# Weights of a column transform by one radix-two step, and the opening of the kernel in a new order

## The chip, the cores and the metric

The kernel runs on one core of one Trainium2 chip. The metric is device time in microseconds (us) for one execution of the whole program. The engines are named as in the profile: PE is TensorE's matmuls and PEld its weight loads, DVE is VectorE, ACT is ScalarE, POOL is GpSimd, and SP is SyncE, which only issues DMAs. "SPq", "ACTq" and "POOLq" are DMA issues on the queues of those engines.

## The reference

```python
def _attn_ref(x):                                  # x: 8 x 3008 x 256
    X = np.fft.fft(x, axis=1)
    X = np.fft.fft(X, axis=2)
    return X.real.astype(np.float32)

def _moe_ref(x, w_in, w_out):                      # w_in: 256 x 2048, w_out: 2048 x 256
    h = x @ w_in
    g = h * np.cos(h)
    return (g @ w_out).astype(np.float32)

def reference(x, moe_w_in, moe_w_out):
    X = _attn_ref(x)                               # real part of a 2-D transform of each batch
    return _moe_ref(X.reshape(8 * 3008, 256), moe_w_in, moe_w_out)
```

A two-dimensional Fourier transform (along the sequence and along the 256 columns), its real part, and then two matrix products with g = h cos(h) between them. All is float32.

## The kernel before, in words

**The column transform is put into the weights.** The transform along the 256 columns is linear, so the kernel does not apply it to the data: it multiplies w_in by the matrix of cosines and sines once, at the start. The results are WC (cosine part) and WS (sine part), each 128 x 2048. Because of the symmetry of the cosine only 128 of the 256 output columns d are kept, and the data z is folded to the same 128 columns. The remaining column, d = 128, gives one extra row of weights; it is computed in row 0 of WS (the sine of d = 0 is nothing). This row has to become a column: tile `wn` (128 x 16) holds it with the hidden units on the partitions. `send_wn` stores 512 of its elements to DRAM (tile `wd`) and then clears row 0 of WS on POOL; `load_wn` loads them back, element by element, spread over the partitions. Until it is there, `seed` (on ACT) cannot start a step that uses it.

The weights are made in four quarters of 512 hidden units. `load_w(q)` brings a quarter of w_in as two halves of 128 rows each (tile `wr`), `weights(e, q)` multiplies both halves by the table CS and adds them up in one PSUM bank (two matmuls, e = 1 for sine, 0 for cosine), and `keep_weights` copies the bank to WS or WC. The quarter 0 is made before the main loop, quarter 1 partly before it, and quarters 2 and 3 inside its first half-steps.

**The sequence transform** of a batch goes in two stages. In the opening, for batch 0, `fold` adds and subtracts mirrored columns of x (DVE), `first_half` multiplies by small tables into the bank `pz`, ACT copies the bank to `zs`, `store_z` writes it to DRAM (`zd`) and `load_z` reads it back in another order as `z`. `second_half` then makes `pb`, which ACT copies to `pq`, the input of the main loop. For later batches the same is done beside the main loop: `fold_x`, `pair_half`, `keep_z` (an ACT copy from PSUM), `fold_z` (one POOL operation for sums, one for differences), `store_pair`, `load_z`.

**The main loop** runs over 384 steps (8 batches x 6 groups of up to 256 positions x 8 blocks of 256 hidden units); each step has two half-steps of 128 hidden units. A half-step makes h with two matmuls (`mm1` with WC and WS, onto a bank that `seed` has prepared), and then ACT and DVE compute g (`act_e`, `dve_h`, `act_round`, `dve_frac`, `act_sin`, `dve_g`). Per step POOL forms combinations of g (`sums`, tile S), and seven matmuls (`mm2`) multiply g and S by w_out or by combinations of w_out (tile VX, made by `combine_w2` on POOL). The second product of a step follows its first by five half-steps.

**What sets the order.** Everything is in a hand-written order: each engine and each DMA queue runs its instructions in the order in which the program issues them (the program turns the automatic scheduler off), and waits between engines are by semaphore. So an instruction that waits holds up all that stands behind it on its engine or queue. `keep_busy` issues matmuls whose result nobody uses.

In the opening POOL's stream holds, in this order: loads of x and CS, small copies, a load of a piece of BJ, the load of w_in's quarter 1, the loads of the first half of z, the clearing of row 0 of quarter 0, the first two loads of w_out (`load_w2(0, 2)` and `(2, 4)`), the clearing of row 0 of quarter 1, and then `combine_w2`. SP's stream holds the x loads, the stores of z, quarter 0, its share of the z loads, quarter 2, `wn` of quarter 0, quarter 3, and then the rest of z's stores, w_out, BJ and z.

Of the kernel before, what the change touches and what calls it, by code (L numbers as in the profile page):

```python
# [33 lines left out]
def _consts():  # L34
# [57 lines left out]

    c = np.arange(ND)
    d = np.arange(128)
    ang = 2.0 * np.pi * np.outer(c, d) / ND
# [36 lines left out]
def kernel(  # L132
# [88 lines left out]

    CS = cpool.tile([128, 512], FP, tag="CS", name="CS")
    wr = {
# [4 lines left out]
    def raw(q, i):  # L228
        return wr[q][:, 512 * i : 512 * i + 512]
# [6 lines left out]
    def load_cs(eng):  # L236
        eng.dma_start(
            out=CS.rearrange("p (i d) -> p i d", i=2),
            in_=CS_dr.ap().rearrange("(i p) d -> p i d", p=128),
        )  # L240

# [24 lines left out]
    for c in parts[:2]:  # L266
        load_x(c, 1, nc.scalar)
    WC = cpool.tile([128, NDFF], FP, tag="WC", name="WC")
    WS = cpool.tile([128, NDFF], FP, tag="WS", name="WS")
# [43 lines left out]
    def first_half(c):  # L313
# [34 lines left out]
        nc.scalar.copy(out=zps[p][:, 512 * q : 512 * q + 512], in_=pz)  # L348

# [37 lines left out]
    def fold_ends(e):  # L387
        lo, hi = xz[:, 1:128], xz[:, 255:128:-1]
        at = 129 if e else 1
        nc.gpsimd.tensor_tensor(  # L390
            out=xzf[:, at : at + 127], in0=lo, in1=hi, op=ALU.subtract if e else ALU.add
        )
        if e:
            small.append(dict(out=xzf[:, 0:129:128], in_=xz[:, 0:129:128]))
# [12 lines left out]
    def keep_z(b, p, q, pz):  # L407
        if q == 0:
            zrs[b, p] = spool.tile([128, XP * ND], FP, tag="xp", bufs=4, name="zr")
        nc.scalar.copy(out=zrs[b, p][:, 512 * q : 512 * q + 512], in_=pz)  # L410

    def fold_z(b, p, e):
        if e == 0:
            zfs[b, p] = spool.tile([128, 1024], FP, tag="zs", bufs=2, name="zs")
        zr = zrs[b, p][:, 0:1024].rearrange("y (i d) -> y i d", d=ND)
        zv = zfs[b, p].rearrange("y (e i d) -> y e i d", e=2, d=128)
        nc.gpsimd.tensor_tensor(
            out=zv[:, e, :, 1:128],
            in0=zr[:, :, 1:128],
            in1=zr[:, :, 255:128:-1],  # L420
            op=ALU.subtract if e else ALU.add,
        )

# [66 lines left out]
    def load_z(b, half, j0=0, j1=NJ, engs=(nc.sync, nc.sync)):  # L490
        if b not in z2s:
            z2s[b] = spool.tile([128, NJ * 128], FP, tag="z2", bufs=1, name="z2")
        for e in range(2):
            for r in range(2):
                p0 = 64 * e + 32 * half + 16 * r
                f0 = 256 * j0 + r * 128 * (j1 - j0)
# [93 lines left out]

    def weights(e, n, tag="M", pw=None, both=(0, 1)):
        pw = pw or psum("pw", tag)
        for i in both:
            nc.tensor.matmul(  # L594
                pw,
                lhsT=CS[:, 256 * i + 128 * e : 256 * i + 128 * e + 128],
                rhs=raw(n, i),
                start=(i == 0),
                stop=(i == 1),
            )  # L600
        return pw
# [4 lines left out]

    wds = {}

    def send_wn(n):
        row = WS[0:1, 512 * n : 512 * n + 512]  # L610
        wds[n] = dpool.tile([1, 512], FP, tag="wd", bufs=3, name="wd")
        nc.scalar.dma_start(out=wds[n], in_=row)
        nc.gpsimd.memset(row, 0.0)

    def load_wn(n, eng=nc.sync):
        eng.dma_start(
            out=wn[:, 4 * n : 4 * n + 4], in_=wds[n].rearrange("o (k p) -> (o p) k", p=128)
        )

    class Step:  # L620
        pass

    VX = cpool.tile([128, 4 * 1024], FP, tag="VX", name="VX")
    ident = cpool.tile([128, 128], FP, tag="ident", name="ident")
# [296 lines left out]
    copy_v = nc.vector.tensor_copy  # L921
    pds = [psum("pd", tag) for tag in ("H", "H", "M")]
    for pd in pds:
# [44 lines left out]
    for half in range(2):  # L968
        load_z(0, half, 4)
    nc.sync.dma_start(out=L2, in_=L2_dr.ap())  # L970
    opening = {
        0: ((combine_w2, 0, 2), (combine_w2, 2, 4)),
        2: ((load_bj, 512, NJ * 64),),
        3: ((combine_w2, 4, 6, 0, 2),),
        4: ((combine_w2, 4, 6, 2, 4),),
        5: ((combine_w2, 6, 8, 0, 2),),
# [25 lines left out]
    pbs = [psum("pb", "M"), borrow("pb", 1)]  # L1002
# [138 lines left out]
```

## Time and profile before

| | us |
|---|---|
| median of three runs (1918.94 to 1920.99) | 1919.08 |
| the profiled execution, its own time | 1920.06 |
| span of the profiled execution | 1918.3 |
| last matmul starts before / first DMA issue of the last output | 1912.7 / 1913.0 |
| first 26.8 us: TensorE busy | 22.8 |
| 26.8 to 54 us: TensorE busy | 25.7 of 27.2 |
| 54 to 110 us: TensorE busy | 56.0 of 56.0 |

The span is the time from the first to the last instruction that the profiler recorded. "Busy" of an engine is the time in which it has an instruction at work; since matmuls overlap, a busy TensorE is not one at its peak, but idle time of TensorE is time in which nothing was there for it to do. The groups of instructions that cost most of TensorE's time are the second product (L778) and the first (L687):

```profile
L778 PE MATMUL M<-S,VX 128*128 128x256 f32 (+1 forms) x2304 | 626.2, 377 | 0.0
L687 PE MATMUL H<-pq,WC 128*128 128x256 f32 (+1 forms) x1536 | 452.7, 376 | 1.5 <-ACT H L668 1.5
L687 PE MATMUL H<-pq,WS 128*128 128x256 f32 (+1 forms) x1536 | 450.9, 375 | 0.0
```

A row reads: line, engine, operation, output<-inputs, shapes, count, then busy us and mean ns of one, then the idle time of the engine just before them and what ended it. A float32 matmul shows as two records.

### The profile page before, as it was taken

What the parts mean: (1) busy time and instruction counts of PE and PEld (TensorE: products, weight loads), DVE (VectorE), ACT (ScalarE), POOL (GpSimd) and SP (SyncE); (2) the same over time, 40 slices, a digit from 0 to 9 for tenths busy, and PEclk for the clock granted to TensorE, in tenths of its full rate; (3) what the DMA queues carried; (4) which work ended last, traced back from release to release, by engine and by line L of the source; (5) the groups of instructions that cost most, each with busy time, mean ns of one, the idle gap of its engine ahead of it and who ended that gap; (6) DMA issues with size and microseconds to landing.
All of it is one profiled execution on the core that took longest, in us unless ns stands there. A gap on an engine that the chain in (4) does not pass through costs nothing.

```text
span 1918.3 us, 32225 instructions
## 1 busy us (share of the span) xinstructions
PE 1906.3 (99%) x10392; PEld 1660.1 (87%) x10392; DVE 1463.5 (76%) x2538; ACT 1494.6 (78%) x3354; POOL 1431.4 (75%) x1711
## 2 busy tenths in 40 slices
PE   9999999999999999999999999999999999999998
PEld 5888889888888889888898888988889888898887
DVE  5777777777777787777777777777777777788787
ACT  3777778778787787778777787778777887788775
POOL 5778768887688776887668776788867788666775
PEclk9999999999999999999999999999999999999999
DMA  7712225022240223311242212512116121210001
GB/s 214 158 29 37 46 55 127 19 42 39 66 110 19 41 42 95 78 32 33 37 115 61 38 25 42 137 35 42 28 34 151 24 41 26 40 24 15 12 15 30
DMA packets 172811, 108.11 MB, mean 56 GB/s; under 512 B 113506, under 2 KB 152256, under 8 KB 171572
## 3 DMA queue, kind: packets, MB, share of 16 engines
q1 hardware_dynamic: 168612, 101.75, 23.8%
q0 software_dynamic: 1120, 3.01, 0.5%
q10 hardware_dynamic: 2912, 1.29, 0.3%
q8 instruction: 84, 1.38, 0.3%
q14 instruction: 83, 0.68, 0.1%
HBM read 68.72 MB, written 48.40 MB: 61 GB/s over the span
## 4 chain that ended last, share of the span: by engine, by line
PE 89%; SPq 4%; DMA 3%; POOL 3%; issue 1%; DVE 1%; ACT 0%; DVEq 0%; ACTq 0%; POOLq 0%
PE M L778 53%; PE H L687 30%; DMA xp<-in_x_dram 2%; PE pz L399 2%; SPq L210 2%; PE pb L512 2%; SPq L916 1%; POOL xf L376 1%; SPq L217 1%; PE pz L325 1%; DMA xp<-xr 0%; DMA wn<-wd 0%; POOL S L745 0%; PE pw L594 0%; POOL S L751 0%
## 5 line engine op out<-in xcount | busy, mean ns | idle before, releaser
L745 POOL TENSOR_TENSOR S<-r 128x512 f32<-128x512 f32 (+1 forms) x383 | 475.5, 1242 | 389.7 <-DVE r L729 335.5
L725 ACT ACTIVATE r<-r 128x512 f32<-128x512 f32 (+1 forms) x768 | 476.5, 620 | 245.3 <-DVE r L719 243.8
L719 DVE SCALAR_TENSOR_TENSOR r<-r,H 128x512 f32<-128x512 f32 (+1 forms) x768 | 518.9, 676 | 158.2 <-ACT r L715 132.2
L778 PE MATMUL M<-S,VX 128*128 128x256 f32 (+1 forms) x2304 | 626.2, 377 | 0.0
L729 DVE SCALAR_TENSOR_TENSOR r<-H,r 128x512 f32<-128x512 f32 (+1 forms) x768 | 518.9, 676 | 122.9 <-ACT r L725 79.1
L778 PEld LDWEIGHTS M<-S,VX 128*128 128x128 f32 x2304 | 433.4, 190 | 72.0 <-issue 22.7
L687 PE MATMUL H<-pq,WC 128*128 128x256 f32 (+1 forms) x1536 | 452.7, 376 | 1.5 <-ACT H L668 1.5
L687 PE MATMUL H<-pq,WS 128*128 128x256 f32 (+1 forms) x1536 | 450.9, 375 | 0.0
L715 ACT ACTIVATE r<-H 128x512 f32<-128x512 f32 (+1 forms) x768 | 447.4, 583 | 0.2 <-DVE H L703 0.2
L703 DVE TENSOR_TENSOR H<-ew,H 128x256 f32<-128x256 f32 (+1 forms) x768 | 325.0, 423 | 152.6 <-PE H L687 92.6
L778 PE MATMUL M<-r,w 128*128 128x256 f32 (+1 forms) x1536 | 387.6, 375 | 0.0
L668 ACT ACTIVATE H<-nb,wn 128x256 f32<-128x256 f32 (+1 forms) x766 | 365.7, 477 | 4.6 <-DMA wn<-wd 2.0
L699 ACT ACTIVATE ew<-H 128x256 f32<-128x256 f32 (+1 forms) x768 | 288.1, 375 | 102.8 <-PE H L687 97.0
L687 PEld LDWEIGHTS H<-pq,WC 128*128 128x128 f32 x1536 | 283.9, 190 | 47.2 <-ACT H L668 8.4
L778 PEld LDWEIGHTS M<-r,w 128*128 128x128 f32 x1536 | 300.3, 196 | 27.6 <-issue 0.5
L687 PEld LDWEIGHTS H<-pq,WS 128*128 128x128 f32 x1536 | 290.2, 190 | 34.6 <-issue 2.4
L751 POOL TENSOR_TENSOR S<-S,r 128x256 f32<-128x256 f32 (+1 forms) x383 | 275.9, 720 | 30.0
L752 POOL TENSOR_TENSOR S<-r,S 128x256 f32<-128x256 f32 (+1 forms) x383 | 275.3, 719 | 30.0
L778 PE MATMUL M<-r,VX 128*128 128x256 f32 (+1 forms) x768 | 225.2, 375 | 0.0
L778 PE MATMUL M<-S,w 128*128 128x256 f32 (+1 forms) x768 | 225.2, 375 | 0.0
L778 PEld LDWEIGHTS M<-S,w 128*128 128x128 f32 x768 | 150.4, 196 | 14.6
L778 PEld LDWEIGHTS M<-r,VX 128*128 128x128 f32 x768 | 145.8, 190 | 14.6
(87 smaller groups left out, 875.0 us busy)
## 6 DMA issues: line engine op xcount, KB each, us to landing
out_dram<-ob SPq DMA_DIRECT2D x724, 32.0 KB
xp<-in_x_dram SPq DMA_DIRECT2D x119, 128.0 KB
xp<-xr SPq DMA_DIRECT2D x112, 128.0 KB
z<-zd SPq DMA_DIRECT2D x56, 192.0 KB
xr<-in_x_dram SPq DMA_DIRECT2D x14, 752.0 KB
zd<-zs SPq DMA_DIRECT2D x98, 96.0 KB
nb<-nd SPq DMA_DIRECT2D x23, 256.0 KB
wr<-in_moe_w_in_dram SPq DMA_DIRECT2D x3, 512.0 KB
```

Of the source, the lines that this page charges most:

```text
L668: nc.scalar.activation(out=h.H[:, 0:T], in_=s.nb[:, 0:T], func=AF.Copy, bias=0.25, scale=wn[:, f : f + 1])
L687: nc.tensor.matmul(h.H[:, 0:T], lhsT=W[:, 128 * f : 128 * f + 128], rhs=s.pq[:, e * 256 : e * 256 + T], start=False, stop=True, skip_group ...
L699: nc.scalar.mul(out=h.ew[:, 0:T], in_=h.H[:, 0:T], mul=2.0)
L703: nc.vector.tensor_tensor(out=h.H[:, T : 2 * T][:, ::-1], in0=h.ew[:, 0:T], in1=h.H[:, 0:T], op=ALU.subtract)
L715: nc.scalar.activation(out=r, in_=y, func=AF.Copy, bias=BIG, scale=1.0)
L719: nc.vector.scalar_tensor_tensor(out=r, in0=r, scalar=-BIG, in1=y, op0=ALU.add, op1=ALU.subtract)
L725: nc.scalar.activation(out=r, in_=r, func=AF.Sin, bias=0.0, scale=SIN_SCALE)
L729: nc.vector.scalar_tensor_tensor(out=r, in0=y, scalar=-0.25, in1=r, op0=ALU.add, op1=ALU.mult)
L745: tt(out=sv[:, 0:2], in0=qv[:, 1:2].to_broadcast([128, 2, T]), in1=qv[:, 0:4:3], op=ALU.subtract,)
L751: tt(out=sv[:, 2], in0=sv[:, 1], in1=gv[:, 0, 0], op=ALU.subtract)
L752: tt(out=sv[:, 3], in0=gv[:, 1, 0], in1=sv[:, 2], op=ALU.add)
L778: nc.tensor.matmul(acc[key][m // 2][:, 256 * (m % 2) : 256 * (m % 2) + T], lhsT=w, rhs=a, start=first, stop=s.fp == 7, skip_group_check=True,)
```

## The change

The change has four parts.

1. The column transform of w_in takes one step of radix two. For an even column d the rows c and c + 128 of the table are equal, for an odd d they are opposite. So `mix_weights` first forms the sum and the difference of the two halves of a quarter (512 columns each), and `weights` multiplies the sum by the even columns of the table (64 of them) and the difference by the odd ones, into the two halves of a bank: two matmuls with 64 columns of weights, where two with 128 columns were. CS shrinks from 128 x 512 to 128 x 256. Quarters 0 and 1 are mixed on DVE, quarters 2 and 3 on POOL. As the 128 columns d now stand in the order even, then odd, the data has to stand in it too: ACT's copies of `pz` read every other column (`first_half`, `keep_z`), and `fold_z` and `fold_ends` need two POOL operations where one was.
2. `turn_wn` replaces the way of the column over DRAM: four matmuls with row 0 of WS as weights (one row, 128 columns) and a single one as input give four columns of a bank, which `keep_wn` copies to `wn` on DVE. Row 0 of WS is cleared on POOL after that.
3. Quarter 1 of w_in is loaded by SP behind the loads of z, not by POOL ahead of them; its product and that of all later quarters stand in the first half-steps.
4. The opening is reordered: one more `keep_busy` bank at the start, three more such matmuls around the first products, `load_w2(0, 2)` and `(2, 4)` issued inside the loop's first half-steps, and z's later columns loaded in two parts (4 to 8 and 8 to 24, the second at step 4).

```diff
-    c = np.arange(ND)
-    d = np.arange(128)
+    c = np.arange(128)
+    d = np.concatenate([np.arange(0, 128, 2), np.arange(1, 128, 2)])
...
-        nc.scalar.copy(out=zrs[b, p][:, 512 * q : 512 * q + 512], in_=pz)
+        nc.scalar.copy(
+            out=zrs[b, p][:, 512 * q : 512 * q + 512].rearrange("y (i o m) -> y i o m", o=2, m=128),
+            in_=pz.rearrange("y (i m o) -> y i o m", o=2, m=128),
+        )
...
-        nc.gpsimd.tensor_tensor(
-            out=zv[:, e, :, 1:128],
-            in0=zr[:, :, 1:128],
-            in1=zr[:, :, 255:128:-1],
-            op=ALU.subtract if e else ALU.add,
-        )
+        for o in range(2):
+            k = 1 - o
+            nc.gpsimd.tensor_tensor(
+                out=zv[:, e, :, o, k:64],
+                in0=zr[:, :, o, k:64],
+                in1=zr[:, :, o, 127 : 64 - o : -1],
+                op=ALU.subtract if e else ALU.add,
+            )
...
+    def mix_weights(n, o, eng):
+        to = mixed(n, o)
+        a, b = raw(n, 0), raw(n, 1)
+        if n not in (1, 2):
+            a, b = (t.rearrange("p (v c) -> p v c", v=2) for t in (a, b))
+        eng.tensor_tensor(out=to, in0=a, in1=b, op=ALU.subtract if o else ALU.add)
+
-    def weights(e, n, tag="M", pw=None, both=(0, 1)):
+    def weights(e, n, tag="M", pw=None):
         pw = pw or psum("pw", tag)
-        for i in both:
+        for o in range(2):
+            at = 128 * e + 64 * o
             nc.tensor.matmul(
-                pw,
-                lhsT=CS[:, 256 * i + 128 * e : 256 * i + 128 * e + 128],
-                rhs=raw(n, i),
-                start=(i == 0),
-                stop=(i == 1),
+                pw[64 * o : 64 * o + 64],
+                lhsT=CS[:, at : at + 64],
+                rhs=mixed(n, o),
+                start=True,
+                stop=True,
             )
...
-    def send_wn(n):
-        row = WS[0:1, 512 * n : 512 * n + 512]
-        wds[n] = dpool.tile([1, 512], FP, tag="wd", bufs=3, name="wd")
-        nc.scalar.dma_start(out=wds[n], in_=row)
-        nc.gpsimd.memset(row, 0.0)
-
-    def load_wn(n, eng=nc.sync):
-        eng.dma_start(
-            out=wn[:, 4 * n : 4 * n + 4], in_=wds[n].rearrange("o (k p) -> (o p) k", p=128)
-        )
+    def turn_wn(n, pw):
+        for k in range(4):
+            f = 512 * n + 128 * k
+            nc.tensor.matmul(
+                pw[:, k : k + 1],
+                lhsT=WS[0:1, f : f + 128],
+                rhs=ones[0:1, 0:1],
+                start=k == 0,
+                stop=True,
+                skip_group_check=True,
+            )
+        nc.gpsimd.memset(WS[0:1, 512 * n : 512 * n + 512], 0.0)
+
+    def keep_wn(n, pw):
+        copy_v(out=wn[:, 4 * n : 4 * n + 4], in_=pw[:, 0:4])
...
-    pds = [psum("pd", tag) for tag in ("H", "H", "M")]
+    pds = [psum("pd", tag) for tag in ("H", "H", "H", "M")]
...
-    load_w(1, nc.gpsimd)
+    for o in range(2):
+        mix_weights(0, o, nc.vector)
     load_z(0, 0, 0, 4, (nc.gpsimd, nc.gpsimd))
     store_z(3, 0, 4, (nc.sync, nc.scalar))
     load_z(0, 1, 0, 4, (nc.sync, nc.scalar))
+    load_w(1)
+    store_z(1, 4)
     load_w(2)
-    pw = [psum("pw", "H") for _ in range(2)]
-    for e in (1, 0):
-        weights(e, 0, pw=pw[e])
-    keep_weights(1, 0, pw[1], copy_v)
+    store_z(2, 4)
+    load_w(3)
+    keep_busy(pds[0], 512, False)
+    pw = [weights(1, 0)]
+    keep_weights(1, 0, pw[0], copy_v)
     copy_v(out=wrow, in_=WS[0:1, 0:256])
-    keep_weights(0, 0, pw[0], copy_v)
-    send_wn(0)
-    load_w2(0, 2, nc.gpsimd)
-    load_w2(2, 4, nc.gpsimd)
-    load_wn(0)
-    load_w(3)
-    fold_weights(1, 1, "M", copy_v)
-    send_wn(1)
-    store_z(1, 4)
-    load_wn(1)
-    for p in (2, 0, 3):
+    pw.append(weights(0, 0, "H"))
+    keep_weights(0, 0, pw[1], copy_v)
+    keep_busy(pds[0], 512, False)
+    turn_wn(0, pw[0])
+    keep_wn(0, pw[0])
+    keep_busy(pds[0], 256, False)
+    for p in (0, 3):
         store_z(p, 4)
...
-    pw = [weights(0, 1, both=(0,))]
+    for o in range(2):
+        mix_weights(1, o, nc.vector)
...
-                    if h is cur:
-                        weights(0, 1, pw=pw[0], both=(1,))
...
-        if k in (1, 2, 3, 4):
-            pw.append(weights(*((1, 2), (0, 2), (1, 3), (0, 3))[k - 1]))
+        if k < 5:
+            pw.append(weights(*((1, 1), (0, 1), (1, 2), (0, 2), (1, 3))[k]))
+        if k == 4:
+            pw.append(weights(0, 3))
+        if k in (1, 3, 5):
+            turn_wn(k // 2 + 1, pw[k + 1])
...
-        if k in (1, 2, 3, 4, 5):
-            e, q = ((0, 1), (1, 2), (0, 2), (1, 3), (0, 3))[k - 1]
-            keep_weights(e, q, pw[k - 1], copy_v)
-        if k in (2, 5):
-            send_wn(2 if k == 2 else 3)
-        elif k in (4, 7):
-            load_wn(2 if k == 4 else 3, nc.scalar)
+        if k < 6:
+            e, q = ((1, 1), (0, 1), (1, 2), (0, 2), (1, 3), (0, 3))[k]
+            keep_weights(e, q, pw[k + 2], copy_v)
+        if k in (1, 3, 5):
+            keep_wn(k // 2 + 1, pw[k + 1])
+        if k == 1:
+            load_w2(0, 2, nc.gpsimd)
+        if k < 2:
+            for o in range(2):
+                mix_weights(2 + k, o, nc.gpsimd)
```

More of the change, by code (lines that the diff above doesn't have):

```diff
@@ L220, in load_xx @@
                     )
-    CS = cpool.tile([128, 512], FP, tag="CS", name="CS")
+    CS = cpool.tile([128, 256], FP, tag="CS", name="CS")
     wr = {
@@ L236, in load_cs @@
     def load_cs(eng):
[L237 to L240 removed]
+        eng.dma_start(out=CS, in_=CS_dr.ap())
     def load_w(q, eng=nc.sync, i0=0, i1=2):
@@ L267 @@
         load_x(c, 1, nc.scalar)
+    VX = cpool.tile([128, 4 * 1024], FP, tag="VX", name="VX")
     WC = cpool.tile([128, NDFF], FP, tag="WC", name="WC")
@@ L347, in first_half @@
             zps[p] = spool.tile([128, m], FP, tag=tag, bufs=n, name="zs")
-        nc.scalar.copy(out=zps[p][:, 512 * q : 512 * q + 512], in_=pz)
+        nc.scalar.copy(
+            out=zps[p][:, 512 * q : 512 * q + 512].rearrange("y (i o m) -> y i o m", o=2, m=64),
+            in_=pz.rearrange("y (i m o) -> y i o m", o=2, m=64),
+        )
     zps = {}
@@ L387, in fold_ends @@
     def fold_ends(e):
-        lo, hi = xz[:, 1:128], xz[:, 255:128:-1]
-        at = 129 if e else 1
-        nc.gpsimd.tensor_tensor(
-            out=xzf[:, at : at + 127], in0=lo, in1=hi, op=ALU.subtract if e else ALU.add
-        )
+        at = 128 * e
+        for o, k in ((1, 64), (2, 1)):
+            nc.gpsimd.tensor_tensor(
+                out=xzf[:, at + k : at + (128 if o == 1 else 64)],
+                in0=xz[:, o:128:2],
+                in1=xz[:, 256 - o : 128 : -2],
+                op=ALU.subtract if e else ALU.add,
+            )
         if e:
@@ L409, in keep_z @@
             zrs[b, p] = spool.tile([128, XP * ND], FP, tag="xp", bufs=4, name="zr")
-        nc.scalar.copy(out=zrs[b, p][:, 512 * q : 512 * q + 512], in_=pz)
+        nc.scalar.copy(
+            out=zrs[b, p][:, 512 * q : 512 * q + 512].rearrange("y (i o m) -> y i o m", o=2, m=128),
+            in_=pz.rearrange("y (i m o) -> y i o m", o=2, m=128),
+        )
     def fold_z(b, p, e):
@@ L414, in fold_z @@
             zfs[b, p] = spool.tile([128, 1024], FP, tag="zs", bufs=2, name="zs")
-        zr = zrs[b, p][:, 0:1024].rearrange("y (i d) -> y i d", d=ND)
-        zv = zfs[b, p].rearrange("y (e i d) -> y e i d", e=2, d=128)
-        nc.gpsimd.tensor_tensor(
-            out=zv[:, e, :, 1:128],
-            in0=zr[:, :, 1:128],
-            in1=zr[:, :, 255:128:-1],
-            op=ALU.subtract if e else ALU.add,
-        )
+        zr = zrs[b, p][:, 0:1024].rearrange("y (i o m) -> y i o m", o=2, m=128)
+        zv = zfs[b, p].rearrange("y (e i o m) -> y e i o m", e=2, o=2, m=64)
+        for o in range(2):
+            k = 1 - o
+            nc.gpsimd.tensor_tensor(
+                out=zv[:, e, :, o, k:64],
+                in0=zr[:, :, o, k:64],
+                in1=zr[:, :, o, 127 : 64 - o : -1],
+                op=ALU.subtract if e else ALU.add,
+            )
     def patch_z(b, p):
@@ L589, in fold_weights, with mixed @@
         keep_weights(e, n, weights(e, n, tag), copy)
-    def weights(e, n, tag="M", pw=None, both=(0, 1)):
+    def mixed(n, o):
+        if n in (1, 2):
+            at = 0 if o else 1024
+            return wr[n][:, at : at + 512]
+        at = 512 if n == 0 else 768
+        return VX.rearrange("p (v c) -> p v c", v=4)[:, 2 * o : 2 * o + 2, at : at + 256]
+    def mix_weights(n, o, eng):
[5 more added lines that the diff above has]
+    def weights(e, n, tag="M", pw=None):
         pw = pw or psum("pw", tag)
-        for i in both:
+        for o in range(2):
+            at = 128 * e + 64 * o
             nc.tensor.matmul(
-                pw,
-                lhsT=CS[:, 256 * i + 128 * e : 256 * i + 128 * e + 128],
-                rhs=raw(n, i),
-                start=(i == 0),
-                stop=(i == 1),
+                pw[64 * o : 64 * o + 64],
[3 more added lines that the diff above has]
+                stop=True,
             )
@@ L968 @@
     for half in range(2):
-        load_z(0, half, 4)
+        load_z(0, half, 4, 8)
     nc.sync.dma_start(out=L2, in_=L2_dr.ap())
     opening = {
-        0: ((combine_w2, 0, 2), (combine_w2, 2, 4)),
+        0: ((load_w2, 2, 4, nc.gpsimd), (combine_w2, 0, 2)),
+        1: ((combine_w2, 2, 4),),
         2: ((load_bj, 512, NJ * 64),),
         3: ((combine_w2, 4, 6, 0, 2),),
-        4: ((combine_w2, 4, 6, 2, 4),),
+        4: ((combine_w2, 4, 6, 2, 4), (load_z, 0, 0, 8), (load_z, 0, 1, 8)),
         5: ((combine_w2, 6, 8, 0, 2),),
@@ L1001 @@
         nc.vector.memset(h.H[:, 0 : h.s.T], 0.25)
-    pbs = [psum("pb", "M"), borrow("pb", 1)]
+    pbs = [borrow("pb"), borrow("pb", 1)]
     first = second_half(0, (0,), pbs)
```

7 lines of the change are left out of this document (2 added, 5 removed).

## The prediction

> **What bounds the kernel now.** I read the page first (busy times), then the stretches, then the waits and the chain of waits of the opening, then POOL's timeline and the DMA issues there.
>
> ```profile
> PE 1906.3 (99%) x10392; PEld 1660.1 (87%) x10392; DVE 1463.5 (76%) x2538; ACT 1494.6 (78%) x3354; POOL 1431.4 (75%) x1711
> ```
>
> The second line is one row of the table by stretches (from:to, then busy us and count of PE, PEld, DVE, ACT, POOL, granted clock, DMA share, GB/s):
>
> ```profile
> 110.00:1905.00 1795.00, 1794.60 (x9791) 1576.41 (x9790) 1388.39 (x2402) 1426.49 (x3201) 1352.82 (x1592) 1.00 0.22 50
> ```
>
> TensorE is the limit. From 110 to 1905 us it is idle for 0.4 us of 1795 at a granted clock of 1.00, so nothing that is done on ACT, POOL, DVE or a queue there is paid for unless it makes TensorE wait. The instructions of TensorE after the opening are the same in both kernels. What can move is the opening:
>
> ```profile
> 20.94 3.38 DMA zd<-zs
> ...
> 24.75 1.82 DMA z<-zd
> 26.57 0.24 issue
> 26.81 0.91 PE pb L512 x32
> 27.72 1.06 PE pw L594 x2
> ...
> 33.69 1.72 PE pw L594 x4
> ...
> 41.39 8.70 DMA wn<-wd
> 50.08 0.02 issue
> 50.11 0.46 ACT H L668
> ```
>
> This is the chain of waits, each piece with start, length and what it was. The first z comes over DRAM and opens the second transform (pb) at 26.81. Then the products with w_in (pw, 1.72 us for the four records of one 128x512 result) stand in TensorE's stream, and at 49.08 it runs dry for 1.53 us because the column wn of the third quarter took 8.70 us through DRAM:
>
> ```profile
> PE H L687 <- ACT H L668: 1.5, 1, 1.5
> ...
> PE pb L512 <- DMA z<-zd: 0.8, 1, 0.8
> ```
>
> I use three marks of before: A = 26.81 (pb starts), B = 42.83 (first `M<-r,w`, the second product of step 0), C = 53.00 (that of step 2). From C on TensorE never waits. The change is worth what it does to C.
>
> **The change part by part.**
>
> *The product with w_in halves in depth.* Each of the eight results was two 128-wide matmuls (1.72 us); now it is two 64-wide ones over 128 rows that write the two halves of a bank. The trace has that shape in the first transform:
>
> ```profile
> 17.84 1.41 PE L325 MATMUL pz<-xf,L 96*64 96x512 f32 x4
> 18.75 0.23 PE L337 MATMUL pz<-xf,L 96*64 96x4 f32 x2
> ```
>
> Its chain piece is 1.08 us for such a pair, so I take 1.08: overlap of the two column halves is part of that row. Bounds: 0.86 (one 128-wide matmul, half of 1.72) and 1.72 (no overlap).
>
> *Turning the column.* Four matmuls per quarter with one row of weights and one output column replace store, load and wait. No row has it. The one-row `H<-pq,wrow` takes 0.57 us for two records where the 128-row one takes 0.38, so 0.095 us of each of its weight loads is uncovered; a four-column matmul adds 0.03 a record (0.06 for two, L337). 8 records x 0.125 = 1.0 us a quarter. Bounds: 8 x 0.03 = 0.24 (load covered) and 8 x (0.182 + 0.03) = 1.7 (the whole load of a one-row weight, 182 ns, uncovered). I take 1.0, since the wrow row has the same shape of weights. [...]
>
> *Mark A.* w(0) has landed at 20.49. DVE then makes two sums (nearest row: 96x508, 0.68 us): 21.85. TensorE, under cover of a keep-busy matmul, does two results (2 x 1.08), keep-busy 0.86, turn 1.0, keep-busy 0.43: 26.35. z: its store took 3.38 us while the second quarter (512 KB, POOL, 19.07) was in flight; that load moves behind z, and the shortest store-to-z landing in the trace view of zd is 2.6, so z lands between 25.8 and 26.57. I take the early end, the load being gone: A = 26.35, gain 0.46. The fourth opening matmul (0.86) ends before 7.3 and pushes the first pz some 0.7 us, but the third waits until 11.80 for x anyway: nothing, 0.7 if that cover were gone. CS, POOL's load at 15.33, is half as large. On SP the quarter 1 load costs one issue (0.43, row of wr) ahead of the later z stores, which wait behind nothing now that wn's two loads (0.38 and 1.62) are gone from that queue; ACT's queue loses its six issues for wd and wn.
>
> *A to B (16.02 before).* pb 0.91; the wait for ACT's copy of pb, which a product covered before, 0.40; three WC/WS products and pn 4 x 0.38; two wrow 2 x 0.57; together 3.97. Then six results 6 x 1.08, eight WS/WC products 8 x 0.38, two turns 2 x 1.0: 11.5. In all 15.5: gain 0.5. The sums they need: quarter 1 on DVE ahead of its first `H` subtraction (w(1) by SP behind z, landing near 28, needed near 30); quarters 2 and 3 on POOL, 2 x 1.27 each.
>
> *B to C (10.17 before).* Two steps of 4.19 = 8.38; the wait for wn goes (1.79 with its restart); the third turn adds 1.0; and the bank of step 0's fifth product is freed only by DVE's copy of wn(3): after WS, DVE needs 0.40 + 0.69 + 0.15, TensorE has 0.76 of other work: 0.48. Sum 9.86: gain 0.3.
>
> Without a new wait C = 51.7, gain 1.3.
>
> *The new wait.* POOL was free early; now it is a chain:
>
> ```profile
> 27.43 1.57 POOL L257 DMA_DIRECT2D w<-in_moe_w_out_dram  x2
> 29.00 0.52 POOL L613 MEMSET WS<- 1x512 f32 x1
> 35.41 1.42 POOL L653 TENSOR_TENSOR VX<-w 128x256 f32<-128x256 f32 x2 [5.89 <-DMA w<-in_moe_w_out_dram]
> ```
>
> and of its DMA issues (last column: us from issue to landing):
>
> ```profile
> w<-in_moe_w_out_dram POOLq DMA_DIRECT2D x2, 512.0 KB, 8.2
> ...
> wr<-in_moe_w_in_dram POOLq DMA_DIRECT2D x1, 512.0 KB, 4.9
> ```
>
> w_out's first part was issued at 27.43. It now stands behind the clearing of WS row 0 for quarter 1, which waits for the second turn: A + 3.97 + 1.08 + 0.76 + 1.08 + 1.0 = 34.2, memset 0.52, issue at 34.8. Queued behind it on POOL: quarter 3's sums, the second part's issue, combine 2.92 (35.41 to 38.33), sums of step 0 2.55 (41.65 to 44.20), memset 0.52, combine 2.92, and the first sum of step 1, 1.06. If w_out lands at L, that sum is there at L + 9.97; TensorE wants it 1.52 into step 1, and C follows 2.67 later: C = L + 12.64 when this binds, from L = 39.1 on. Landing after issue: 4.9 (one 512 KB load) to 8.2 (two side by side, with the wn loads ahead of w(3)); low end 2.7 (BJ, 128 KB). One load, no wn loads: I take 4.9, L = 39.7, C = 52.3, a wait of 0.6. [...]
>
> *Steady state.* 56 ACT copies of pz (0.58 us) now read every other column; the one row with a stride of two, `ob<-po`, has 0.61. 56 folds on POOL (1.26) become two each: one more start, some 0.2 (64x4: 0.205). Held against each other in the timeline, POOL's sums end 1.9 us or more before TensorE reads them everywhere after 60 us, and ACT's seeds about as far ahead: that slack hides both. Exposed they would cost up to 56 x 0.2 = 11. The last two thirds of z are loaded later, behind x of the next batch: transfers end by 90 us, and the first need is step 13.
>
> Sum: -0.5 - 0.5 - 0.3 + 0.6 = -0.7 us. The profiled execution took 1920.06 us (span 1918.3), 1.0 above the median of 1919.08; against the median: **1918.4**.
>
> **The rivals.**
> *Late w_out (the other side).* L at 34.8 + 8.2 = 43.0 gives C = 55.6: slower by 2.6, 1921.7. It decides from L = 40.4, 5.6 us after issue. For: the only w_out row is 8.2, and stores of z and w_out's third part are in the queues then. Against: that row had two loads and 4-byte wn loads about. 0.25.
> *Cheap turns, early z.* A turn at 0.24 makes POOL's issue 1.5 earlier, z at 25.3 another 0.5: 32.8; landing 4.0: C = 49.4, faster by 3.6, 1915.5 (a little more if 2.7 holds). For: the lower bounds are from rows. Against: all must hold. 0.22.
> *The halves don't overlap.* 1.72 a pair: two more before A and six after, 8 x 0.64 = 5.1 less the 1.3: slower by 3.8, 1922.9. Against: the pz row. 0.05.
> *The steady state pays.* 28 pairs x 0.3 = 8.4: 1927. Against: that slack. 0.05.
> My forecast 0.43, own range 1917.0 to 1919.8.
>
> **How the numbers follow.** 0.2% is 3.8 us, about what a measurement of this kernel can tell from no change. Faster by more: some half of the cheap-turn case, 0.12. Slower by more: the last two and the tail of late w_out, 0.11. Within: 0.77. The range, 1915.3 to 1921.8, takes in both main rivals.
>
> **What would show it.** Right: no store or load of wn; pw in 1.08 us; no wait of ACT's seed for wn; pb near 26.3; POOL's combine waiting for w_out near 39.7 and TensorE idle under 1 us on S in the second step; 110 to 1905 as full as before. Wrong: turns far from 1.0 us, w_out landing before 38 or after 40.4, DVE's sums of quarter 1 holding its queue, or any idle time of TensorE in the steady state.

## The result and the profile after

| | before | after |
|---|---|---|
| median of 16 runs each, us | 1919.2 (1918.49 to 1922.07) | 1923.33 (1920.74 to 1925.41) |
| ratio to before | | 1.002 (95% interval 1.0013 to 1.0028) |
| profiled execution / span, us | 1920.06 / 1918.3 | 1922.86 / 1921.1 |
| mark A, pb starts | 26.81 | 25.42 (forecast 26.35) |
| mark B, first second-product of step 0 | 42.83 | 41.65 (forecast 41.84) |
| mark C, that of step 2 | 53.00 | 56.63 (forecast 52.3) |
| runs with a mean granted clock of 0.998 or less | a few (5 of 93 in the experiments) | 16 of 16 |

The change made the kernel slower by 0.2%, some 4 us; forecast was 0.7 us less than before. The three marks say where: the kernel is 1.2 us ahead at B and 3.6 behind at C. After C the distance shrinks a little, to 2.85 us at the last matmul. The busy line and the stretch from 110 to 1905 us of the changed kernel show that the main loop hardly moved:

```profile
PE 1909.9 (99%) x10432; PEld 1663.2 (87%) x10432; DVE 1466.0 (76%) x2546; ACT 1493.9 (78%) x3354; POOL 1443.4 (75%) x1784
```

```profile
110.00:1905.00 1795.00, 1793.60 (x9794) 1576.95 (x9793) 1388.07 (x2402) 1427.45 (x3208) 1360.62 (x1658) 1.00 0.23 50
```

TensorE is busy 1793.60 us there, where it was 1794.60. So look between B and C. The chain of waits of the changed kernel around B (start, length, what it was):

```profile
32.92 0.99 PE pw L634 x8
...
33.96 0.47 POOL WS L642
34.43 7.09 DMA w<-in_moe_w_out_dram
...
41.60 2.10 POOL VX L679 x3
...
44.56 1.12 PE M L804 x2
```

The turn of quarter 1's column (L634) is followed by the clearing of the row on POOL (L642), then by the issue of w_out's first part, which takes 7.09 us to land, then by POOL's combinations (L679), for which TensorE waits. TensorE's timeline (start, length, what, and in brackets the idle time before it and what ended it) puts a number on the wait:

```profile
41.65 1.01 PE L804 MATMUL M<-r,w 128*128 128x225 f32 x4
44.56 1.12 PE L804 MATMUL M<-r,VX 128*128 128x225 f32 x2 [1.90 <-POOL VX L679]
45.61 1.86 PE L634 MATMUL pw<-ones,WS 1*128 1x1 f32 x8
```

The wait is 1.90 us. But look at the durations behind it: two records of a second product take 1.12 us, and the eight of a turn 1.86, where the turn at 32.85 took 1.05. The table by stretches (busy us and count of PE, PEld, DVE, ACT, POOL, then granted clock, DMA share, GB/s) says why:

```profile
41.04:44.45 3.41, 1.60 (x8) 0.69 (x4) 1.57 (x3) 1.00 (x3) 2.77 (x4) 1.00 0.80 229
44.45:51.27 6.82, 6.71 (x20) 5.62 (x21) 1.98 (x5) 1.14 (x3) 6.58 (x10) 0.50 0.61 168
```

For 6.82 us after the wait TensorE was granted half its clock. In the profile of before, the wait for wn of 1.53 us (49.08 to 50.61) cost no clock.

SP's timeline of the changed kernel shows what is under way beside that load:

```profile
33.73 1.23 SPq L254 DMA_DIRECT2D w<-in_moe_w_out_dram  x1
...
35.74 0.43 SPq L254 DMA_DIRECT2D w<-in_moe_w_out_dram  x1
```

**The theory that follows.** Two terms, one behind the other. (1) w_out's first part takes 2.2 us longer to land than the forecast's 4.9, because SP's loads of its third and fourth part are under way beside it, one issued 0.7 us before it and one 1.3 us after it. (2) The wait that this makes is followed by a stretch at half clock. By the forecast's own formula, C = landing + 12.64, the late landing alone gives 41.52 + 12.64 = 54.16; the measured 56.63 is 2.47 more, which I take as the price of the clock. (Half of 6.82 us would be 3.41. Part of that is hidden: the wait of 0.41 us for DVE's copy of wn, for one, which e2 and e8 below show at full clock, is not in this trace.) **Rivals**: the load is slow by itself (or by the stores of z); the wait alone costs, and the clock is incidental; the turns cost more than their rows show.

### The profile page after: what moved, and what is told of

Its sections match the earlier page's. It is cut to its first block, busy times and chain, and to the rows that moved or that the text cites. A ratio compares the mean times of both kernels' runs of the same rounds, so it can differ in the third digit from the quotient of the medians.

```text
span 1921.1 us, 32387 instructions
## 1 busy us (share of the span) xinstructions
PE 1909.9 (99%) x10432; PEld 1663.2 (87%) x10432; DVE 1466.0 (76%) x2546; ACT 1493.9 (78%) x3354; POOL 1443.4 (75%) x1784
## 4 chain that ended last, share of the span: by engine, by line
PE 90%; DMA 3%; SPq 3%; POOL 2%; DVE 1%; issue 1%; ACT 0%; DVEq 0%; POOLq 0%
PE M L804 54%; PE H L713 31%; DMA xp<-in_x_dram 2%; PE pz L403 2%; PE pb L521 2%; SPq L210 1%; SPq L942 1%; PE pd L659 1%; POOL xf L377 1%; PE pz L323 0%; DMA xp<-xr 0%; SPq L217 0%; DMA w<-in_moe_w_out_dram 0%; DMA out_dram<-ob 0%; DVE ob L924 0%
```

## The experiments

All ran beside the kernel before on the same chip, with 11 timed runs each. In the tables, "C" is the mark of the profiled run against 53.00, and "clock lost" counts the timed runs with a mean granted clock of 0.998 or less. One lost stretch of 6.83 us at half clock lowers the mean over 1920 us by 0.0018, so the count separates them, if roughly: a lost stretch of 3.41 us (0.0009) can escape it, and every mean also holds some us at half clock behind the last matmul (3.3 to 6.3 us in the traces).

### Is the late landing made by SP's own loads?

`e9_wout_sp_late`: the changed kernel with SP's two loads of w_out behind its loads of z.

```diff
-    load_w2(4, 6)
     load_bj(256, 512)
-    load_w2(6, 8)
     for half in range(2):
         load_z(0, half, 4, 8)
+    load_w2(4, 6)
+    load_w2(6, 8)
```

> The changed kernel with SP's loads of w_out's third and fourth part moved behind its loads of z's columns 4 to 8; nothing else. Theory (the 7.09 us from issue to landing of POOL's load of w_out's first part come from SP's two loads of 512 KB that stand in front of it on the DMA engines): it lands within 3.5 to 5 us of its issue at 34.4, so by 38 to 39.4; C = L + 12.64 no longer binds or just does, TensorE's wait on VX in step 0's products is under 0.4 us, C between 51.5 and 52.3, median 1918.5 to 1920 (the one-row products after pb can still lose the clock in some runs). Rival (the load is slow by itself, or by the stores of z): lands at 7 us or more after issue as before, wait of 1.9, C 54.2 or 56.6 with the clock lost, median 1921.5 to 1923.5. A third way: the later third part of w_out lands too late (after 46) and a wait before step 2's products takes the place.

`e10_sp_late_fill`: the same, with one useless matmul of 256 columns between pb and the wait for ACT's copy of it.

```diff
     first = second_half(0, (0,), pbs)
+    nc.tensor.matmul(pw[0][:, 0:256], lhsT=WC[:, 0:128], rhs=WC[:, 0:256],
+                     start=True, stop=True, skip_group_check=True)
     for e in range(2):
         keep_b((0,), first[0], e, pbs[e])
```

> The same, with one useless 256-column matmul in the wait for ACT's copy of pb. If what is left of the loss in the kernel above is the clock lost after pb in some runs: granted clock full in more of the runs, median 0.3 to 1 us below the kernel above, about 1918.9. If that stretch doesn't matter here: the same median within 0.3 us.

| | median us | ratio to before (95%) | C | clock lost |
|---|---|---|---|---|
| e9_wout_sp_late | 1920.53 | 1.0009 (1.0000 to 1.0018) | -0.29 | 3 of 11 |
| e10_sp_late_fill | 1919.56 | 1.0001 (0.9992 to 1.0010) | -0.30 | 0 of 11 |

POOL's timeline of e9_wout_sp_late:

```profile
35.04 0.80 POOL L254 DMA_DIRECT2D w<-in_moe_w_out_dram  x1
...
40.07 1.41 POOL L679 TENSOR_TENSOR VX<-w 128x256 f32<-128x256 f32 x2 [0.97 <-DMA w<-in_moe_w_out_dram]
```

The same load, issued 0.6 us later, now lands 5.0 us after its issue, and TensorE's wait of 1.90 us is gone. This is shown: SP's two loads were the delay. (SP's loads of z, of 32 KB each, come forward into their place, and the landing is short all the same.) Because the issue came later than forecast, the landing is at 40.1 and not before 39.4, and C is 52.71, which is 0.4 above the upper end expected. The stores of z stayed where they were, so they were not the cause of the excess. The median of e9 is 0.5 above its expectation; 3 of 11 runs lost the clock (up to 1926.75), and the other eight alone have a median of 1920.0. With the useless matmul (e10) none fell to 0.998, and the median is 1.0 lower, as expected.

### Is it the wait, or the clock after it?

`e2_fill_wait`: the changed kernel with two useless matmuls of 512 columns at the place of the wait. They do not shorten the wait; they only keep TensorE at work in it. `e8_fill_both` has a third one after pb. The expectations call the theory of the two terms W; G is that the clock is lost behind pb too in some runs, and that a useless matmul there makes this rarer.

```diff
+            if k == LAG:
+                mm2(done, 0, 2)
+                for _ in range(2):
+                    nc.tensor.matmul(pw[6], lhsT=WC[:, 0:128], rhs=WC[:, 0:512],
+                                     start=True, stop=True, skip_group_check=True)
+                mm2(done, 2, 3)
+            else:
                 mm2(done, 4 * v, 4 * v + (1 if pair or double else 3), order)
```

> Edit: the changed kernel with two 512-column matmuls of no use put into the place where TensorE waits for the combination of w_out (behind the second w_out product of step 0, before the third; they write a bank of which only four columns are written anew and used later). Nothing else moves, w_out lands as late as before. Theory W: the 1.9 us of waiting are filled with 1.7 us of matmuls, so nothing is lost by them, but the granted clock stays at 1.00; the turn and the products behind the wait take 0.98 and 0.38 us again and not 1.79 and 0.75, step 2 starts near 54.1 in place of 56.6, and the time falls by some 2.5 us to about 1920.8. [...] Rival P (POOL's late chain is all there is, the clock only fills time that TensorE would wait anyway): the clock is full but step 2 stays within 0.5 us of 56.6.

> Edit: the kernel of e2 (the wait for w_out filled with two 512-column matmuls, w_out as late as in the changed kernel) with a 512-column matmul behind pb as well (0.86 us, of which 0.4 lies in a wait). Theory G: both places that can lose the clock are filled, so every run is at full clock: step 2 near 54.2 (0.4 over e2's profile), the spread of the runs falls from 5 us to about 1 or 2, and the median from e2's 1922.1 to about 1920.3, though the kernel does 0.4 us more. Rival: the spread and the median of e2 stay (1922 to 1922.6): what separates e2's runs is not the clock behind pb.

| | median us | ratio to before (95%) | w_out lands | landing + 12.64 | C measured | clock lost |
|---|---|---|---|---|---|---|
| after | 1923.33 | 1.0020 (1.0013 to 1.0028) | 41.52 | 54.16 | 56.63 | 16 of 16 |
| e2_fill_wait | 1922.14 | 1.0016 (1.0007 to 1.0025) | 40.99 | 53.63 | 53.82 | 7 of 11 |
| e8_fill_both | 1921.98 | 1.0013 (1.0004 to 1.0022) | 43.32 | 55.96 | 55.99 | 0 of 11 |

TensorE's timeline of e2_fill_wait shows the useless pair, the turn at its normal length, and C:

```profile
42.67 1.88 PE L1068 MATMUL pw<-WC 128*128 128x512 f32 x4
...
44.86 1.05 PE L634 MATMUL pw<-ones,WS 1*128 1x1 f32 x8
...
53.82 0.93 PE L804 MATMUL M<-r,w 128*128 128x225 f32 x4
```

With the clock kept, C is 2.81 us earlier than in the changed kernel, though w_out landed only 0.53 earlier: the clock is a term of its own. The formula agrees to 0.03 us in e8. In e2 it agrees to 0.19, but that shows nothing: POOL's sum of step 1 was ready when TensorE came for it (no idle time before it), and C was set by TensorE's own work, the useless pair included. Why does the median of e2 gain only 1.2? Seven of its runs still lost the clock. The four at 0.999 or more took 1920.18 to 1921.13, near what the late landing alone should cost (1919.08 + 1.16 = 1920.2); the others took 1921.92 to 1925.17. In e8 no run fell to 0.998, but the expected median of 1920.3 was missed by 1.7: pb started 0.6 us later than in e2 and the useless matmul behind it took up 0.4 more, so that w_out was issued at 35.53, behind both of SP's loads (33.76 and 35.50), and landed 7.8 us later:

```profile
35.53 0.80 POOL L254 DMA_DIRECT2D w<-in_moe_w_out_dram  x1
...
43.40 1.40 POOL L679 TENSOR_TENSOR VX<-w 128x256 f32<-128x256 f32 x2 [3.82 <-DMA w<-in_moe_w_out_dram]
```

So e8 gives back by the later landing much of what it saves on the clock: its C is 0.64 and its median 1.35 us under the changed kernel's. The landing times follow SP's two loads: 5.0 us with neither of them ahead (e9), 6.3 and 7.1 with one issued before and one behind (e2 and the changed kernel), 7.8 with both before (e8).

### Another queue for w_out

`e1_wout_pool_early` issues w_out's first two parts on POOL right after the first turn; `e3_wout_act` issues them on ACT's queue in half-steps 0 and 1; `e5_act_fill_pb` is e3 with the useless 256 columns after pb.

```diff
     keep_wn(0, pw[0])
+    load_w2(0, 2, nc.gpsimd)
+    load_w2(2, 4, nc.gpsimd)
...
-        0: ((load_w2, 2, 4, nc.gpsimd), (combine_w2, 0, 2)),
+        0: ((combine_w2, 0, 2),),
...
-        if k == 1:
-            load_w2(0, 2, nc.gpsimd)
```

The two lines added for e3 and e5 in place of e1's first two:

```diff
         if k < 2:
+            load_w2(2 * k, 2 * k + 2, nc.scalar)
```

> Edit: the changed kernel with the first two loads of w_out (0:2 and 2:4) issued by POOL right after the first column is turned, as the kernel before has them, and not behind quarter 1's clearing. [...] Rival D (an early w_out only pushes quarters 2 and 3 of w_in back): TensorE waits 1 us or more for POOL's sums of quarter 2 near 34.8, time 1920 to 1922.

> Edit: the changed kernel with w_out's first two parts issued by ACT's queue in the first two half-steps (near 30 and 32.5 us), so that they stand behind nothing on POOL and behind w_in's quarters 1 and 2 on the DMA engines. Theory W: w_out 0:2 lands near 36, before 39.1, so no wait for the combination and no half clock; step 2 near 51.7 to 52, time 1917.5 to 1918.5. [...] Rival Q (ACT's issue of 0.4 us each holds up its seeds and rounding): TensorE waits for ACT's seed near 31, time 1919 to 1920.

> Edit: the kernel of e3 (w_out's first two parts from ACT's queue) with one 256-column matmul of no use right behind pb, where TensorE waited 0.46 us for ACT's copy of pb. In e1's and e3's profiles the granted clock fell to half for one window of 3.41 us right behind the stretch of pb, that wait and the one-row products. [...]

| | median us | ratio to before (95%) | C | clock lost |
|---|---|---|---|---|
| e1_wout_pool_early | 1921.28 | 1.0007 (0.9998 to 1.0016) | +1.08 | 6 of 11 |
| e3_wout_act | 1919.70 | 1.0004 (0.9995 to 1.0012) | +0.92 | 4 of 11 |
| e5_act_fill_pb | 1918.87 | 1.0000 (0.9991 to 1.0009) | +1.34 | 2 of 11 |

In all three TensorE no longer waits for w_out, and the time is that of before, no better; the 1918 to 1919 expected of e1 and the 1917.5 to 1918.5 of e3 were missed. The profiled runs of all three lost the clock, at another place. TensorE's timeline of e3_wout_act after pb, then its table by stretches:

```profile
27.07 0.65 PE L713 MATMUL H<-pq,WC 128*128 128x225 f32 x2 [0.46 <-ACT pq L537]
27.64 0.64 PE L700 MATMUL H<-pq,wrow 1*128 1x225 f32 x2
...
30.39 1.98 PE L618 MATMUL pw<-wr,CS 128*64 128x512 f32 x4
```

```profile
26.79:30.20 3.41, 3.13 (x12) 1.85 (x12) 1.38 (x2) 1.56 (x5) 0.00 (x0) 1.00 0.87 276
30.20:33.61 3.41, 3.41 (x10) 1.48 (x8) 1.57 (x4) 1.00 (x2) 2.44 (x2) 0.50 0.93 306
```

A wait of 0.46 us and three products with a single row of weights (two with `wrow` and the one for `pn`), and the next 3.41 us run at half clock: a pair of w_in's products takes 1.98 us where it takes 1.08. The wait is not needed for that loss. In e5 the useless matmul fills it, and the profiled run lost the clock all the same, behind a stretch with the same three products in which TensorE was never idle:

```profile
27.55:30.96 3.41, 3.41 (x15) 1.98 (x16) 1.50 (x3) 1.39 (x5) 0.00 (x0) 1.00 0.88 291
30.96:34.37 3.41, 3.41 (x10) 1.27 (x8) 1.81 (x4) 0.84 (x2) 2.52 (x2) 0.50 0.93 309
```

So the useless matmul makes the loss rarer and does not exclude it: without it (e3, e9 and e11 below) 12 of 33 runs lost the clock, with it (e5, e10 and e6) 2 of 33. The changed kernel has these products in a row too (and idle 0.38 at 26.24), because the products of quarter 1 with w_in that stood between them before now stand after them. e4 below keeps those products there, and lost the clock in none of 11 runs. That speaks for the products with one row of weights as the cause, but it is not shown: no run changed them alone, and the profiled runs of e6 and e8 kept the clock behind a stretch that holds the same three. That of e8 differs from e5's by some 0.1 us of its content:

```profile
27.72:31.13 3.41, 3.41 (x15) 1.90 (x15) 1.18 (x3) 1.31 (x4) 0.00 (x0) 1.00 0.93 298
```

### What do the turns cost?

`e4_turn_only`: the kernel *before*, with nothing but the column's way over DRAM replaced by the turns, quarter 0's before pb and the others in half-steps 1, 3 and 5:

```diff
-    send_wn(0)
+    turn_wn(0, pw[1])
+    keep_wn(0, pw[1])
...
+        if k in (1, 3, 5):
+            turn_wn((1, 2, 3)[k // 2], pw11 if k == 1 else pw[k - 2])
...
-        if k in (2, 5):
-            send_wn(2 if k == 2 else 3)
-        elif k in (4, 7):
-            load_wn(2 if k == 4 else 3, nc.scalar)
+        if k in (1, 3, 5):
+            keep_wn(k // 2 + 1, pw11 if k == 1 else pw[k - 2])
```

`e6_dram_3`: e5 with quarter 3's column sent over DRAM again, on ACT's queue; `e7_dram_23`: quarter 2's as well (stored in half-step 2, loaded in 4, cleared in 6); `e11_dram_3_nofill`: e6 without the useless matmul.

```diff
-        if k in (1, 3, 5):
+        if k in (1, 3):
             turn_wn(k // 2 + 1, pw[k + 1])
...
+        if k == 5:
+            send_wn(3)
+        if k == 8:
+            load_wn(3)
+        if k == 9:
+            nc.gpsimd.memset(WS[0:1, 512 * 3 : 512 * 3 + 512], 0.0)
```

> Edit: the kernel before with one part of the change alone: its column of weights is turned by TensorE (four one-column matmuls a quarter, 0.98 us in the changed kernel's trace) in place of the way over DRAM; products, order of loads and everything else as before. By the price of the turns: one turn before pb (pb starts some 0.3 to 1.0 us later), three behind it at 1.0 us each, and the 1.8 us of the wait for wn gone: step 2 near 54.5 in place of 53.0, slower by some 1.5 us, 1920.5. Rival (the wait for wn was the whole cost and the turns hide beside other work): step 2 near 51.5, time 1917.7.

> Edit: the kernel of e5, with the column of the last quarter (3) taken over DRAM again and not turned by TensorE: stored from ACT's queue at half-step 5, loaded at 8, needed at 11. Price of a turn as read so far: 0.98 us, 0.10 of a weight load uncovered behind it, and 0.41 us of waiting for its copy. Theory: step 2 earlier by 1.5 us than in e5 (near 50.7 at full clock), median some 1.5 us under e5's. Rival (turns lie beside waits that would be there anyway, for POOL's sums of step 1): step 2 earlier by 0.5 us or less.

> Edit: the kernel of e6, with quarter 2's column over DRAM too (stored at half-step 2, loaded at 4, needed by ACT's seed at 7, as in the kernel before). Theory (price of a turn): another 1.1 us less than e6, step 2 near 49.6 at full clock. Rival (the way over DRAM is as long as before, 8.7 us from load to landing, so the wait of the kernel before for the third quarter comes back, and with a shorter stream in front of it is longer): TensorE waits 1 us or more for ACT's seed near 47, no gain over e6 or a loss.

> The kernel that was fastest so far (w_out's first two parts loaded from ACT's queue, the last quarter's column over DRAM, a useless matmul after pb) without the useless matmul. If the matmul kept the clock: some 3 or 4 of 11 runs at a mean clock of 0.998 or less, median 1918.0 to 1918.5. If the gain is the last turn alone: median 1917.2 to 1917.6, all runs at full clock.

| | median us | ratio to before (95%) | C | clock lost |
|---|---|---|---|---|
| e4_turn_only | 1922.34 | 1.0013 (1.0004 to 1.0022) | +3.06 | 0 of 11 |
| e6_dram_3 | **1917.35** | **0.9988 (0.9979 to 0.9997)** | -2.38 | 0 of 11 |
| e7_dram_23 | 1917.82 | 0.9994 (0.9985 to 1.0003) | -2.25 | 2 of 11 |
| e11_dram_3_nofill | 1918.62 | 0.9998 (0.9989 to 1.0007) | +0.01 | 5 of 11 |

One turn in e4_turn_only, in TensorE's timeline:

```profile
46.69 0.54 PE L781 MATMUL M<-r,VX 128*128 128x225 f32 x2
47.16 1.05 PE L610 MATMUL pw<-ones,WS 1*128 1x1 f32 x8
48.14 0.65 PE L690 MATMUL H<-pq,WS 128*128 128x225 f32 x2
```

From start to start the turn takes 0.98 us, and the product behind it 0.65 instead of 0.54, a tenth more. That is the forecast's 1.0, and in the old order it makes the kernel slower: three turns behind pb come to 3.2 us, and the wait that they remove was 1.5. Another 0.8 of e4's +3.06 is from the opening, where pb starts at 27.62 behind the first turn, and 0.3 from a new wait for DVE at 49.55. That is 2.8; the loss is twice the 1.5 that was expected, and the last 0.3 is not accounted for.

e6_dram_3 is the fastest of all and beats both kernels. Against e5 it gives back one turn, 1.1 us, and the wait of 0.41 us for DVE's copy of wn that stood behind it (47.34 in e3): 1.5, and the medians differ by 1.52. Its stretch from 26.8 to 54 us:

```profile
26.80:54.00 27.20, 27.20 (x133) 19.65 (x133) 19.66 (x39) 17.62 (x43) 21.15 (x27) 1.00 0.75 226
```

TensorE is busy 27.20 of 27.20 us at full clock. Without the useless matmul (e11) C is 2.4 us later in the profiled run, which had half its clock for 6.83 us from 27.26 on; the clock is lost in 5 of 11 runs, and the median is 1.3 higher. A second column over DRAM (e7) brings nothing more. TensorE's timeline of e7_dram_23:

```profile
37.74 0.65 PE L724 MATMUL H<-pq,WC 128*128 128x225 f32 x2 [1.50 <-ACT H L705]
```

ACT issues the store of wd only at 36.94, after it had stood still from 35.57 on, and its seed (L705) is queued behind that: TensorE waits 1.50 us for that seed. The store reads a row of WS that DVE's copy writes from 35.74 to 36.43, so most of the standing still is the wait for that copy. What held the last 0.5 us is not shown.

## Why the prediction was wrong, and where it was right

- **The product with w_in**: 1.08 us forecast, 1.08 for a pair measured (1.01 from start to start). Right.
- **The turns**: 1.0 forecast, 0.98 and a tenth behind it measured. Right, and so the "cheap turns" rival fell. Mark A came 0.93 us before its forecast (whose terms add up to 26.30, not 26.35): quarter 0 of w_in had landed at 19.55, where 20.49 was taken, and from there TensorE's own work led to pb without a wait. Mark B came only 0.2 us early, because A to B took 16.23 in place of 15.5: a WC or WS product beside a turn, a one-row or a 64-wide product takes 0.48 to 0.58 from start to start, where 0.38 was taken. The wait for ACT's copy of pb was as forecast (0.38 against 0.40).
- **The wait for DVE's copy of wn(3)**: 0.48 forecast, 0.41 measured in e1, e2, e3 and e9. Right.
- **POOL's issue of w_out**: 34.8 forecast, 34.43 measured. Right.
- **The step that failed, first term**: "Landing after issue ... One load, no wn loads: I take 4.9, L = 39.7, C = 52.3". It took 7.09, L = 41.52. The 4.9 came from a row with one load of 128 KB in front of it; here two loads of 512 KB were beside it. e9 took them away and measured 5.0. The change had moved POOL's issue in between SP's issues at 33.73 and 35.74, and the forecast named w_out's third part in a rival, but did not let it into the sum. This mis-sized term is worth +1.9 us on C (52.3 to 54.2).
- **The step that failed, second term**: the clock was in no sum at all. The forecast priced a wait at its length. Measured, the wait of 1.90 us was followed by 6.82 us at half clock, 2.47 us more on C. By the forecast's rule the late landing alone would have given 1919.08 + 1.16 = 1920.2, slower but inside the range; the clock puts the result above its end (1921.8), which had been set by the late-w_out rival at its full landing of 8.2 us. The place of the wait was wrong too: expected was a short one for S in the second step, and TensorE waited 1.90 us for VX in the first step and not at all for S.
- **The rival "late w_out"** was half of the mechanism: it decides from L = 40.4, the landing was 41.52, and C = L + 12.64 held to 0.03 us in e8, at full clock. Even there the chain of waits runs through the wait for VX and DVE's copy of wn, and POOL's sum of step 1, on which the formula rests, adds only 0.1; that both ways come to the same is partly luck. The rival's price was too small by the clock.
- **"The halves don't overlap"** fell with the 1.08 us. **"The steady state pays"** fell too: ACT's strided copies of `pz` take 0.575 us (0.576 before). TensorE does wait longer for POOL, 0.24 us instead of 0.07 at one place in six of the batches, 1.0 us in all, but none of these steps is over 0.1 us longer than before. The distance to the kernel before even shrinks, from 3.63 us at C to 2.85 at the end. Of these 0.8 us, 0.7 lie in two steps (at 476.55 and 1142.22 before) that take 5.11 us in the profile of before and 4.75 in that of the changed kernel. e4, whose main loop is that of before, takes 4.75 there as well, so this is no gain of the change; what held these two steps up stays open.

The account in the two profiled runs: 3.63 at C, less 0.8 given back, is the 2.8 by which they differ (1922.86 against 1920.06). The medians differ by 4.1: the profiled run of before is 0.9 above its median, that of the changed kernel 0.5 below. That part of this is clock lost a second time, after pb, in some of the timed runs is likely from e3 and e11, but no trace of such a run was taken.

What the change would be worth without the late load and the lost clock follows from the same rows. Behind pb five products of 1.72 us (8.6) became six of 1.01 (6.1), which saves 2.5, and a wait of 1.5 is gone. Against that stand three turns of 1.08, the wait of 0.41 behind the last, the wait of 0.38 for ACT's copy of pb, which a product covered before, and the slower products beside the narrow ones. In e1 and e3, where w_out is early and the clock is full from 33.9 us on, B to C takes 10.31; behind the changed kernel's B of 41.65 that gives C = 51.96, an estimate. So the gain would be 1.0 on C, and all of it comes from pb, which starts 1.4 earlier. The forecast's 1.3 (C = 51.7) is near that by luck: A came 0.9 earlier than taken, and A to C would have taken 1.2 longer. The gain was lost to one load that moves beside two others (2.2), and to the clock (2.47).

## What to carry to other kernels

When a DMA issue is moved, list what every queue issues in the 5 us before its new place, and take its landing time from a row with the same company; a load moved between two others of its size took 7.1 us where it takes 5.0 without them. Price a wait of TensorE not by its length only: ask whether half clock can follow, and add that (here 2.47 us behind a wait of 1.90); a useless matmul in the gap is a cheap test, and here it brought the runs with a lost clock from 12 of 33 to 2 of 33. And a column that is turned on the engine that sets the time costs its time there (0.98 us from start to start, and a tenth behind it), while the way over DRAM cost nothing where TensorE had other work until the column was there: e6, the fastest kernel here, turns three columns, sends the last one over DRAM and keeps TensorE busy for 27.20 of 27.20 us. Where it had not, as in the kernel before, TensorE waited 1.53 us.

## What was not expected of the hardware

The granted clock did not fall by idle time alone. Its record in the trace begins at 6.90 us in the changed kernel and at 5.50 in the kernel before, and in every kept trace each later change falls a whole number of steps of 3.41 us behind that beginning: after 11 in the changed kernel, after 7 in e1, e3 and e5, after 6 in e11. So one can say what stood in the stretch of 3.41 us ahead of each loss. TensorE was busy for 1.60 us of it in the changed kernel (then 6.82 us at half clock), 2.95 in e11 (6.83), 3.23 in e1, 3.13 in e3 and all of it in e5 (3.41 each). Other stretches, counted off in the same way, held less and kept the clock. In the kernel before, the two that share the wait for wn had 2.62 and 2.67:

```profile
46.46:49.87 3.41, 2.62 (x14) 2.23 (x12) 2.35 (x5) 1.26 (x3) 0.47 (x2) 1.00 0.46 74
49.87:53.28 3.41, 2.67 (x14) 2.61 (x15) 1.65 (x3) 2.59 (x7) 3.25 (x6) 1.00 0.88 124
```

In e7 the whole wait of 1.50 us for ACT's seed lies in one stretch, with 1.91 busy, and the clock stayed full behind it:

```profile
34.92:38.33 3.41, 1.91 (x10) 0.61 (x6) 1.72 (x5) 1.57 (x4) 2.75 (x3) 1.00 0.85 270
```

So busy time alone does not sort the stretches: 1.91 kept the clock, and 3.41 of 3.41 lost it. Nor do the three products with one row of weights, which e1, e3, e5, e6 and e8 all hold: the first three lost the clock behind them, the last two kept it. At half clock the profiled runs spent one of these steps (3.41 us) or two (6.82), and the same kernel loses the clock in some of its timed runs and not in others (3 to 7 of 11 in e1, e2, e3, e9 and e11). How long a gap TensorE can have at full clock does not follow from them either: half clock came behind a gap of 1.90 us in the profiled run of the changed kernel, and all 16 timed runs of that kernel had a mean clock of 0.998 or less; behind one of 1.50 us in e7 and one of 1.53 in the kernel before, the clock stayed full. What a stretch must hold to keep the clock, no run here settles.
